# Two decode layers on one core: w1 streamed in each layer, one pool, and a whole group's K kept across the layers

## The chip, the cores and the metric

The kernel runs on one core of a Trainium2 chip. The metric is the device time of one execution in microseconds; the number shown for a kernel is the median of several executions. All sizes are float32. Where the text says MiB it means 2^20 bytes; GB/s are 10^9 bytes per second.

## The reference

Two layers, each an attention block over a cache and a gated feed-forward block, for four rows of one token each:

```python
def _A_ref(x, k_cache, v_cache, wq, wo):          # B=4, D=512, 32 query heads, 8 groups, 4096 positions, 128 wide
    q = (x @ wq).reshape(B, Sq, Hq, Dh).transpose(0, 2, 1, 3)
    k = jnp.repeat(k_cache, rep, axis=1)
    v = jnp.repeat(v_cache, rep, axis=1)
    p = _softmax(jnp.einsum("bhqd,bhkd->bhqk", q, k) * (Dh ** -0.5), axis=-1)
    o = jnp.einsum("bhqk,bhkd->bhqd", p, v)
    return o.transpose(0, 2, 1, 3).reshape(B, Sq, Hq * Dh) @ wo

def _B_ref(x, w1, w3, w2):                         # F = 1792
    return (_silu(x @ w1) * (x @ w3)) @ w2

x = A_x
x = x + _A_ref(_layernorm(x), k_cache, v_cache, wq, wo)
x = x + _B_ref(_layernorm(x), w1, w3, w2)
x = x + _A_ref(_layernorm(x), k_cache, v_cache, wq, wo)
x = x + _B_ref(_layernorm(x), w1, w3, w2)
```

Both layers read the same caches and the same weights. Each cache is 64 MiB, wq and wo are 8 MiB each, w1, w3 and w2 are 3.5 MiB each.

## The kernel before, in words

**Steps.** A layer goes through the 8 groups; each group has 4 steps of 1024 positions. A step needs 2 MiB of K and 2 MiB of V (all four rows of the batch). The first layer takes the groups 0 to 7, the second 7 to 0, so group 7 (`TURN`) is the last of the first layer and the first of the second. In a step TensorE computes the scores (L320), VectorE takes the maximum (L323), ScalarE the exponent (L340), TensorE turns the result (L346) and multiplies it with V (L370). The scores of the next step stand ahead of the rest of the step before it.

**The tail of a layer.** Behind the last V come the output projection (L397), a layernorm (L252 to L277) and the feed-forward block: w3's first 256 of 448 columns (L413), w1 (L420), w3's other 192 columns (L413), the gate (L423, L425, L428), five transposes (L432 to L434), and w2 in five pieces of 4, 4, 4, 1 and 1 rows (L446). `busy(n)` puts n transposes of a constant on TensorE whose result nobody reads (L246); they stand in the tail between the real operations.

**What is loaded, and in which order.** `plan` is a list of all loads, in the order of need. `pump()` walks it: a load of a weight that has its own home is issued at once; any other takes a place in `free` (first fit) and, when no place is large enough, the walk stops there until `done()` or `vacate()` gives a place back. So the order of the loads never changes, and a late release holds up every load behind it. All loads stand on SyncE's queue (SPq in the profile). Each load also takes one of eight completion semaphores in turn (DMAHW0 to DMAHW7 in the rows of order below), so SyncE issues a load only once the eighth before it has landed.

**Where it lands.** `pages` has 17 places of 512 KiB. wq and wo (but for group 0's share) have homes of their own; in the second layer the parts that are no longer needed are added to `free`. w1 has a home (3.5 MiB), is loaded once in two halves in the first layer (beside groups 2 and 4) and read by both layers. w3 and w2 are streamed through `free` in both layers.

**What is kept for the second layer.** Of group 7's 16 pages of K nine stay in `pages` (`KEPT`: steps 2 and 3 and one page of step 1), and one (`STORED`) is copied to PSUM by ScalarE (L317) and copied back in the second layer (L176). The other six are loaded again. The second layer takes group 7's steps in the order 2, 3, 0, 1.

Of the kernel before, what the change touches and what calls it, by code (L numbers as in the profile page):

```python
# [8 lines left out]
F32 = mybir.dt.float32  # L9
# [14 lines left out]
FJ = F // 4  # L24
FW = (256, FJ - 256)
EPS = 1e-5
SCALE = DH ** -0.5
RT = 4 * U
# [16 lines left out]
def tile_decode_layers(ctx: ExitStack, tc: tile.TileContext, x, kt, v, wq, wo, w1, w3, w2, out):  # L45
# [18 lines left out]


    homes = {"pages": pages, "wq": wq_sb.rearrange("p g k n -> p (g k n)"),
             "wo": wo_sb.rearrange("p g h e -> p (g h e)")}
    free = [("pages", 0, PAGES)]

# [19 lines left out]

    def stream(keys, src, n=None):  # L90
        plan.append((keys, src, len(keys) if n is None else n))

    def keep(dst, src):
        plan.append((None, src, dst))

    def cache(which, layer, g, c, parts=(4,)):
        src = (kt if which == "k" else v)[g, c]
        r = 0
        for n in parts:
            keys = [(which, layer, g, c, r + i) for i in range(n)]  # L100
            if which == "k" and g == TURN and layer and (c, r) in KEPT:
                pass
            elif layer and keys[0] == ("k", layer, TURN, *STORED):
                stream(keys, None)
            else:
                stream(keys, src[:, r * U:(r + n) * U])
            r += n

    def parts_of(which, layer, i, g, c):
        if which == "k" and g == TURN and c == 1:  # L110
            return (2, 1, 1)
        if i == len(orders[layer]) - 1:
            return (2, 1, 1)
        if layer == 0 and i == len(orders[layer]) - 2 and which == "v":
            return (2, 2)
        if layer == 0 and i == 0:
            return (1, 1, 2)
        if layer and i < 4:
            return (2, 2) if (c, 0) not in KEPT or which == "v" else (4,)
        return (4,)  # L120

    def wq_load(a, b):
        keep(wq_sb[:, a:b].rearrange("p g k n -> p (g k n)"), wq[:, a * RT // 2:b * RT // 2])

    def wo_load(a, b):
        keep(wo_sb[:, a - 1:b - 1].rearrange("p g h e -> p (g h e)"), wo[:, a * RT // 2:b * RT // 2])

    for layer in range(LAYERS):
        steps = orders[layer]
        if layer == 0:  # L130
            wq_load(0, 1)
        for i, (g, c) in enumerate(steps):
            if which_parts := parts_of("k", layer, i, g, c):
                cache("k", layer, g, c, which_parts)
            if layer == 0 and c == 1:
                if g in (0, 1, 3, 5):
                    wq_load(*{0: (1, 2), 1: (2, 4), 3: (4, 6), 5: (6, 8)}[g])
                elif g in (2, 4):
                    k = g - 2
                    keep(w1_sb[:, k:k + 2].rearrange("p k f -> p (k f)"), w1[:, k * F:(k + 2) * F])  # L140
            if i:
                cache("v", layer, *steps[i - 1], parts_of("v", layer, i - 1, *steps[i - 1]))
            if layer == 0 and c == 2:
                if g == 0:
                    stream([("wo", 0)], wo[:, 0:RT // 2], 2)
                elif g in (1, 3, 5):
                    wo_load(g, g + 2)
        cache("v", layer, *steps[-1], parts_of("v", layer, len(steps) - 1, *steps[-1]))
        if layer == 0:
            wo_load(TURN, HKV)  # L150
        else:
            stream([("wo", 1)], wo[:, 0:RT // 2], 2)
        for u in range(2):
            for k in (0, 2):
                a = 4 * KC * FW[0] * u + 4 * FW[u] * k
                stream([("w3", layer, u, k), ("w3", layer, u, k + 1)], w3[:, a:a + 8 * FW[u]])
        for i, (a, b) in enumerate(W2_PARTS):
            stream([("w2", layer, i)], w2[:, a * D:b * D], (b - a + 1) // 2)

# [3 lines left out]
    def pump():  # L163
        while state["next"] < len(plan):
            keys, src, n = plan[state["next"]]
            if keys is None:
                nc.sync.dma_start(n, src)
            else:
                got = take(n)
                if got is None:  # L170
                    return
                home, at, _ = got
                dst = homes[home][:, at * U:(at + n) * U]
                if src is None:
                    for i in range(2):
                        nc.scalar.activation(dst[:, i * U // 2:(i + 1) * U // 2], stored[i], AF.Copy)  # L176
                else:
                    width = src.shape[-1]
                    nc.sync.dma_start(dst[:, :width], src)
                    assert width % len(keys) == 0  # L180
                    n = width // len(keys)
                left[state["next"]] = len(keys)
                room[state["next"]] = got
                for i, key in enumerate(keys):
                    where[key] = (dst[:, i * n:(i + 1) * n] if src is not None else dst, state["next"])
# [95 lines left out]
    def project_q(layer, g, xT, rq):  # L281
        pq = misc()

        def product(k):
            for h in range(REP):
                nc.tensor.matmul(pq[32 * h:32 * h + 32, 0, :], xT[:, 32 * k:32 * k + 32],  # L286
                                 wq_sb[:, g, k, h * DH:(h + 1) * DH], start=(k == 0), stop=(k == KC - 1))

        def turn_q():
            pt = misc()  # L290
            nc.tensor.transpose(pt[:, 0, :], q, ident)
            nc.vector.tensor_copy(qT[:, :, 0:REP],
                                  pt[:, 0, :].rearrange("p (h b) -> p b h", h=REP)[:, 0:B, :])

        product(0)
        yield
        product(1)
        yield
        product(2)
        product(3)  # L300
        if layer:
            vacate("wq", 2 * g, 2)
# [90 lines left out]
    def project_o(layer, g, rowsum):  # L393
# [7 lines left out]
        elif layer:  # L401
            vacate("wo", 2 * g - 2, 2)
        nc.vector.scalar_tensor_tensor(x_sb, x_ps, 1.0, x_sb, op0=ALU.mult, op1=ALU.add,
                                       accum_out=rowsum)

    def feed_forward(layer, xT, rstd, rowsum):
        pg, pu = scores(0), scores(1)

        def up(u):
            for k in range(KC):  # L410
                w = loaded("w3", layer, u, k)
                for j in range(4):
                    nc.tensor.matmul(pu[32 * j:32 * j + 32, FW[0] * u:FW[0] * u + FW[u]], xT[:, 32 * k:32 * k + 32],  # L413
                                     w[:, j * FW[u]:(j + 1) * FW[u]], start=(k == 0), stop=(k == KC - 1))
                done("w3", layer, u, k)
# [135 lines left out]
```

## Time and profile before

| what | us |
|---|---|
| median of 3 runs | 724.01 (723.31 to 724.14) |
| the profiled execution, its own time | 723.5 |
| its span, first to last instruction | 721.6 |
| TensorE busy | 472.6 (65%) |
| VectorE busy | 194.8 (27%) |
| ScalarE busy | 120.1 (17%) |
| moved by DMA | 300.67 MB, mean 417 GB/s |

The profiled execution is 0.5 us faster than the median; between its span and its time lie 1.9 us. Busy times overlap, so no engine's sum is the time.

### The profile page before, as it was taken

To read this page: it belongs to the slowest core of one execution; us is meant where nothing else is said; L and a number is where in the kernel's file an instruction comes from. 1 tells how busy PE (TensorE), PEld (TensorE's weight loads), DVE (VectorE), ACT (ScalarE), POOL (GpSimd) and SP (SyncE) were. 2 spreads that over 40 slices of the span, in tenths; PEclk is the share of its full clock that TensorE was granted. 3 is DMA by queue.
4 is the path that set the end of the run, shared out by engine and by line. 5 is a ranking of instruction groups with operands and counts; after the bars stand their busy time and mean duration, and the time that the engine had idled before them with its cause. 6 is when DMAs were issued, how large, how long until landed. Compare 5 with 4: busy or idle time off the path is not lost.

```text
span 721.6 us, 18367 instructions
## 1 busy us (share of the span) xinstructions
PE 472.6 (65%) x8310; PEld 300.5 (42%) x8310; DVE 194.8 (27%) x694; ACT 120.1 (17%) x323; POOL 2.9 (0%) x10
## 2 busy tenths in 40 slices
PE   5664665745566755566678766766667667566778
PEld 3342443423334533334455544444444444344455
DVE  2222122231122312323222432222332232322221
ACT  1111111111011101112121311111111111111121
POOL 0000000000000000000000000000000000000000
PEclk9887688998678968989999999899998988998799
DMA  9999999999999999999999999999999999999995
GB/s 363 427 430 422 430 424 428 425 426 427 428 422 429 426 429 425 428 423 423 412 371 402 424 426 425 428 425 428 423 430 424 427 427 424 427 426 425 423 416 221
DMA packets 25853, 300.67 MB, mean 417 GB/s; under 512 B 2864, under 2 KB 3120, under 8 KB 5936
## 3 DMA queue, kind: packets, MB, share of 16 engines
q1 hardware_dynamic: 25632, 299.45, 98.5%
q8 instruction: 65, 1.06, 0.6%
q14 instruction: 12, 0.10, 0.0%
q10 hardware_dynamic: 144, 0.07, 0.0%
HBM read 299.43 MB, written 0.07 MB: 415 GB/s over the span
## 4 chain that ended last, share of the span: by engine, by line
DMA 81%; PE 16%; DVE 1%; issue 1%; SPq 0%; ACT 0%; DVEq 0%; ACTq 0%
DMA pages<-in_v 44%; DMA pages<-in_kt 28%; PE sums_ps L370 6%; DMA pages<-in_w 5%; PE scores L320 5%; DMA wq_sb<-in_v 4%; PE turned L346 2%; PE misc L286 1%; DVE pT L348 1%; PE sums_ps L446 0%; PE scores L420 0%; DVE stat L323 0%; PE scores L246 0%; PE scores L413 0%; PE sums_ps L397 0%
## 5 line engine op out<-in xcount | busy, mean ns | idle before, releaser
L370 PE MATMUL sums_ps<-pages,pT 128*4 128x128 f32 x3152 | 128.5, 306 | 127.0 <-DMA pages<-in_v 101.1
L320 PE MATMUL scores<-pages,qT 128*32 128x256 f32 x1736 | 125.0, 436 | 56.5 <-DMA pages<-in_kt 49.9
L370 PEld LDWEIGHTS sums_ps<-pages,pT 128*4 128x4 f32 x3152 | 82.0, 94 | 162.5 <-issue 99.4
L340 ACT ACTIVATE p<-scores,stat 128x512 f32<-128x512 f32 x128 | 87.0, 680 | 282.1 <-PE turned L346 220.4
L323 DVE TENSOR_REDUCE stat<-scores 128x1 f32<-128x512 f32 x128 | 88.5, 691 | 139.4 <-PE scores L320 139.3
L320 PEld LDWEIGHTS scores<-pages,qT 128*32 128x32 f32 x1736 | 63.9, 123 | 99.8 <-issue 74.2
L346 PE MATMUL turned<-ident,p 128*128 128x128 f32 x512 | 95.3, 315 | 0.0
L348 DVE COPY pT<-turned 128x64 f32<-128x64 f32 x128 | 28.1, 219 | 245.7 <-PE turned L346 245.5
L346 PEld LDWEIGHTS turned<-ident,p 128*128 128x128 f32 x512 | 61.1, 156 | 47.7 <-issue 44.9
L335 ACT ACTIVATE stat<-stat 128x1 f32<-128x1 f32 x48 | 14.1, 295 | 269.2 <-DVE stat L333 269.2
L370 PE MATMUL sums_ps<-wq_sb,pT 128*4 128x128 f32 x672 | 25.2, 294 | 24.1 <-DMA wq_sb<-in_v 20.0
L370 PEld LDWEIGHTS sums_ps<-wq_sb,pT 128*4 128x4 f32 x672 | 17.1, 91 | 30.6 <-issue 20.3
L286 PE MATMUL misc<-wq_sb,xT 128*32 128x128 f32 x512 | 24.7, 297 | 0.7 <-DVE ve L275 0.4
L340 ACT ACTIVATION_READ_ACCUMULATOR p<-scores,stat 128x1 f32 x128 | 24.5, 192 | 0.0
L397 PE MATMUL sums_ps<-wo_sb,oT 128*4 128x128 f32 x448 | 15.6, 283 | 6.1 <-DVE o L379 5.4
L246 PE MATMUL scores<-ident 128*128 128x128 f32 x104 | 18.1, 300 | 1.9 <-POOL ident masks.py:199 1.4
L286 PEld LDWEIGHTS misc<-wq_sb,xT 128*32 128x32 f32 x512 | 16.6, 120 | 1.2 <-ACT xT L268 0.4
L370 PE MATMUL sums_ps<-wo_sb,pT 128*4 128x128 f32 x272 | 10.8, 284 | 9.5 <-DMA wo_sb<-in_v 8.0
L397 PEld LDWEIGHTS sums_ps<-wo_sb,oT 128*4 128x4 f32 x448 | 10.8, 88 | 11.3 <-DVE o L379 9.9
L381 DVE SCALAR_TENSOR_TENSOR o<-o,stat,sums_ps 128x128 f32<-128x128 f32 x32 | 11.0, 343 | 13.9 <-PE sums_ps L370 13.9
L246 PEld LDWEIGHTS scores<-ident 128*128 128x128 f32 x104 | 11.8, 148 | 5.6 <-issue 2.4
L320 PE MATMUL scores<-wq_sb,qT 128*32 128x256 f32 x192 | 11.5, 380 | 2.3 <-DMA wq_sb<-in_kt 2.3
(81 smaller groups left out, 187.5 us busy)
## 6 DMA issues: line engine op xcount, KB each, us to landing
pages<-in_kt SPq DMA_DIRECT2D x47, 2048.0 KB, 18.9
pages<-in_v SPq DMA_DIRECT2D x43, 2048.0 KB, 19.5
wq_sb<-in_v SPq DMA_DIRECT2D x9, 2048.0 KB, 32.9
wq_sb<-in_kt SPq DMA_DIRECT2D x6, 2048.0 KB, 32.8
pages<-in_v SPq DMA_DIRECT2D x10, 1024.0 KB, 10.2
wo_sb<-in_v SPq DMA_DIRECT2D x4, 2048.0 KB, 34.1
pages<-in_w SPq DMA_DIRECT2D x7, 1024.0 KB, 11.1
pages<-in_kt SPq DMA_DIRECT2D x6, 1024.0 KB, 9.8
```

Of the source, the lines that this page charges most:

```text
L246: nc.tensor.transpose(pt[:, 0:P], ident, ident)
L286: nc.tensor.matmul(pq[32 * h:32 * h + 32, 0, :], xT[:, 32 * k:32 * k + 32], wq_sb[:, g, k, h * DH:(h + 1) * DH], start=(k == 0), stop=(k = ...
L320: nc.tensor.matmul(ps[32 * b:32 * b + 32, r * QC:(r + 1) * QC], qT[:, b, :], t[:, b, :], start=True, stop=True)
L323: nc.vector.tensor_reduce(st["stat"][:, h:h + 1], ps, axis=AX.X, op=ALU.max, negate=True)
L335: nc.scalar.activation(stat[:, 6:7], stat[:, 2:3], AF.Exp, bias=stat[:, 3:4], scale=-1.0)
L340: nc.scalar.activation(st["p"].rearrange("p n s -> p (n s)"), st["ps"][h], AF.Exp, bias=stat[:, 3:4], accum_out=stat[:, 4 + h:5 + h])
L346: nc.tensor.transpose(pt[:, n, :], st["p"][:, n, :], ident)
L348: nc.vector.tensor_copy(pT, pt.rearrange("p n (b h) -> p n b h", b=B)[:, :, :, 0:REP])
L370: nc.tensor.matmul(o_ps[32 * b:32 * b + REP, :], st["pT"][h][:, NT * (r % 2) + n, b, :], t[:, b, n, :], start=(r == 0 and n == 0), stop=(r ...
L381: nc.vector.scalar_tensor_tensor(acc["o"], acc["o"], st["stat"][:, 6:7], o_ps, op0=ALU.mult, op1=ALU.add)
L397: nc.tensor.matmul(x_ps[32 * k:32 * k + B, :], oT[:, h, :], w[:, h, k * P:(k + 1) * P], start=(h == 0), stop=(h == REP - 1))
```

## The change

Five things change together. w1 loses its home and is streamed in both layers behind the last V, in four pieces of 896 KiB (one for each quarter of the 512 inputs), ahead of w3, which now comes in four such pieces too. `pages` (17 places of 512 KiB) becomes `pool` (96 places of 128 KiB, 24 of the old ones), so pieces take what they need in steps of 128 KiB. All of group 7's K but the `STORED` page (now the last of step 3) stays in the pool for the second layer: 15 pages and the one in PSUM, so none is loaded again, and the second layer takes the steps in their plain order. TensorE computes w1's product first, then w3's whole product. And which loads are cut into smaller pieces changes a little: V of the last three steps of the first layer and of the first two of the second.

```diff
-PAGES = 17
+KB = 256
+POOL = 96
 TURN = HKV - 1
-KEPT = {(2, 0): 4, (3, 0): 4, (1, 3): 1}
-STORED = (1, 2)
+STORED = (STEPS - 1, 3)
...
-    pages = const.tile([P, PAGES * U], F32, name="pages")
+    pool = const.tile([P, POOL * KB], F32, name="pool")
...
-    w1_sb = const.tile([P, KC, F], F32, name="w1_sb")
...
-        orders.append([(g, c) for i, g in enumerate(groups)
-                       for c in ((2, 3, 0, 1) if layer and i == 0 else range(STEPS))])
+        orders.append([(g, c) for g in groups for c in range(STEPS)])
...
-    free = [("pages", 0, PAGES)]
+    free = [("pool", 0, POOL)]
...
-                elif g in (2, 4):
-                    k = g - 2
-                    keep(w1_sb[:, k:k + 2].rearrange("p k f -> p (k f)"), w1[:, k * F:(k + 2) * F])
...
-        for u in range(2):
-            for k in (0, 2):
-                a = 4 * KC * FW[0] * u + 4 * FW[u] * k
-                stream([("w3", layer, u, k), ("w3", layer, u, k + 1)], w3[:, a:a + 8 * FW[u]])
+        for name, w in (("w1", w1), ("w3", w3)):
+            for k in range(KC):
+                stream([(name, layer, k)], w[:, k * F:(k + 1) * F])
...
-                    if key[0] == "k" and key[2] == TURN and key[1] == 0:
-                        for (c, r), m in KEPT.items():
-                            if key[3] == c and r <= key[4] < r + m:
-                                where[("k", 1, *key[2:])] = where[key]
-                                kept.add(key)
+                    if key[:3] == ("k", 0, TURN) and key[3:] != STORED:
+                        where["k", 1, *key[2:]] = where[key]
+                        kept.add(key)
...
-        up(0)
-        for k in range(KC):
-            for j in range(4):
-                nc.tensor.matmul(pg[32 * j:32 * j + 32, 0:FJ], xT[:, 32 * k:32 * k + 32],
-                                 w1_sb[:, k, j * FJ:(j + 1) * FJ], start=(k == 0), stop=(k == KC - 1))
+                    nc.tensor.matmul(ps[32 * j:32 * j + 32, 0:FJ], xT[:, 32 * k:32 * k + 32],
+                                     w[:, j * FJ:(j + 1) * FJ], start=(k == 0), stop=(k == KC - 1))
+                done(name, layer, k)
+
+        product("w1", pg)
         gate = work.tile([P, FJ], F32, name="gate", tag="p", bufs=1)
...
-        up(1)
+        product("w3", pu)
```

On SyncE's queue at the turn from the first layer to the second, before (behind wo's last piece; widths are in floats of each of 128 partitions, so 2048 is 1 MiB; `in_w3` is w3 in device memory):

```order
L167 DMA wo_sb_70<-in_wo 128x2048
L179 DMA pages_68<-in_w3 128x2048 x2
L179 DMA pages_68<-in_w3 128x1536 x2
L179 DMA pages_68<-in_w2 128x2048 x3
L179 DMA pages_68<-in_w2 128x512 x2
L179 DMA pages_68<-in_v 128x2048 x2
L179 DMA pages_68<-in_kt 128x2048 x2
L179 DMA wq_sb_69<-in_v 128x2048
L179 DMA pages_68<-in_v 128x2048
L179 DMA pages_68<-in_kt 128x2048
```

The same place after the change:

```order
L154 DMA wo_sb_70<-in_wo 128x2048
L165 DMA pool_68<-in_w1 128x1792 x4
L165 DMA pool_68<-in_w3 128x1792 x4
L165 DMA pool_68<-in_w2 128x2048 x3
L165 DMA pool_68<-in_w2 128x512 x2
L165 DMA pool_68<-in_v 128x2048 x4
L165 DMA pool_68<-in_v 128x4096
L165 DMA pool_68<-in_kt 128x4096
```

Four pieces of w1 stand ahead of w3, the three K pieces of group 7 are gone, and behind w2 come four halves of V and then V of the third step in one piece of 2 MiB. By the pool's bookkeeping the four w3 pieces each take the place of the w1 piece of the same number, the first two of w2 wait for w3's second piece, the last three of w2 and the first V half for w3's fourth, the other V halves for w2's first three pieces, and the 2 MiB V piece for the scores of the second layer's first step.

On TensorE in the feed-forward block of the first layer, before (`scores1` collects w3's product, `scores0` w1's):

```order
L413 MATMUL scores1_3099<-pages_68,xT_3083 32x256 x16
L420 MATMUL scores0_3098<-w1_sb_71,xT_3083 32x448 x16
L413 MATMUL scores1_3099<-pages_68,xT_3083 32x192 x16
L246 MATMUL scores0_3158<-ident_84 128x128 x7
L432 MATMUL turned_3166<-ident_84,gate_3134 128x128 x3
```

The same place after it:

```order
L396 MATMUL scores0_3094<-pool_68,xT_3079 32x448 x16
L396 MATMUL scores1_3095<-pool_68,xT_3079 32x448 x16
L229 MATMUL scores0_3143<-ident_85 128x128 x7
L411 MATMUL turned_3151<-ident_85,gate_3116 128x128 x3
L412 MATMUL turned_3151<-ident_85,gate_3116 128x128
```

w3's product is no longer parted around w1's, and nothing on TensorE stands between the pieces of either weight.

## Rows read from the trace of the kernel before

**Rows 1.** The page: GB/s in 40 slices of the span, and the chain that ended last.
```profile
GB/s 363 427 430 422 430 424 428 425 426 427 428 422 429 426 429 425 428 423 423 412 371 402 424 426 425 428 425 428 423 430 424 427 427 424 427 426 425 423 416 221
DMA 81%; PE 16%; DVE 1%; issue 1%; SPq 0%; ACT 0%; DVEq 0%; ACTq 0%
```

**Rows 2.** Timeline of SyncE's queue near the end: start us, us, what was issued.
```profile
642.20 0.33 SPq L179 DMA_DIRECT2D wq_sb<-in_v  x1
...
656.84 0.33 SPq L179 DMA_DIRECT2D wo_sb<-in_kt  x1
662.53 5.22 SPq L179 DMA_DIRECT2D wq_sb<-in_v  x2
...
682.12 0.33 SPq L179 DMA_DIRECT2D pages<-in_wo  x1
684.61 0.33 SPq L179 DMA_DIRECT2D wq_sb<-in_w  x1
```

**Rows 3.** Timeline of TensorE at the end: start us, us, instructions, [idle before <-what ended it].
```profile
692.11 1.83 PE L370 MATMUL sums_ps<-wq_sb,pT 128*4 128x128 f32 x32 [3.29 <-DMA wq_sb<-in_v]
...
704.68 1.07 PE L413 MATMUL scores<-wq_sb,xT 128*32 128x256 f32 x16
...
706.43 3.19 PE L420 MATMUL scores<-w_sb,xT 128*32 128x448 f32 x32
709.44 1.48 PE L413 MATMUL scores<-wo_sb,xT 128*32 128x192 f32 x32
...
713.04 1.06 PE L446 MATMUL sums_ps<-wo_sb,hT 128*4 128x128 f32 x32
...
716.44 1.06 PE L446 MATMUL sums_ps<-pages,hT 128*4 128x128 f32 x32 [0.18 <-DMA pages<-in_w]
```

**Rows 4.** Windows at the turn and behind it: us, busy by engine, PEclk, DMA share, GB/s.
```profile
374.00:388.00 14.00, 12.87 (x204) 7.85 (x204) 2.56 (x9) 2.40 (x4) 0.55 (x1) 1.00 0.89 344
400.00:420.00 20.00, 16.88 (x361) 11.49 (x354) 8.34 (x29) 5.96 (x17) 0.00 (x0) 1.00 1.01 422
```

**Rows 5.** Timeline at the turn: TensorE's waits for weights, ScalarE, and the second layer's first scores.
```profile
376.62 1.07 PE L413 MATMUL scores<-pages,xT 128*32 128x256 f32 x16 [0.18 <-DMA pages<-in_w]
...
388.35 1.06 PE L446 MATMUL sums_ps<-pages,hT 128*4 128x128 f32 x32 [1.02 <-DMA pages<-in_w]
...
389.92 0.62 PE L446 MATMUL sums_ps<-pages,hT 128*4 128x128 f32 x16
...
392.25 0.28 ACT L268 ACTIVATE xT<-turned 128x128 f32<-128x128 f32 x1 [9.26 <-PE turned L265]
...
395.18 1.94 PE L320 MATMUL scores<-pages,qT 128*32 128x256 f32 x32 [0.27 <-DVE qT L292]
...
399.65 0.60 ACT L176 ACTIVATE pages<-stored 128x512 f32<-128x512 f32 x1 [0.72 <-PE scores L320]
```

**Rows 6.** A load at the turn on SyncE's queue, and half-microsecond windows behind it.
```profile
376.49 0.33 SPq L179 DMA_DIRECT2D pages<-in_w  x1
...
377.00:377.50 0.50, 0.50 (x16) 0.26 (x8) 0.00 (x0) 0.00 (x0) 0.00 (x0) 1.00 0.96 274
...
379.00:379.50 0.50, 0.50 (x12) 0.24 (x8) 0.00 (x0) 0.00 (x0) 0.00 (x0) 1.00 1.05 438
```

**Rows 7.** Windows and TensorE's timeline around two stretches in which it waited.
```profile
22.60:26.60 4.00, 1.77 (x42) 1.22 (x36) 0.58 (x3) 0.78 (x2) 0.00 (x0) 1.00 1.03 438
26.70:30.00 3.30, 0.42 (x5) 0.25 (x9) 0.00 (x0) 0.00 (x0) 0.00 (x0) 0.50 1.00 427
504.50:507.80 3.30, 1.52 (x35) 0.89 (x33) 1.60 (x7) 0.78 (x2) 0.00 (x0) 1.00 0.97 412
508.00:511.00 3.00, 3.00 (x32) 1.52 (x31) 0.69 (x1) 0.00 (x0) 0.00 (x0) 0.50 1.00 423
...
507.88 3.61 PE L320 MATMUL scores<-pages,qT 128*32 128x256 f32 x32 [1.07 <-DMA pages<-in_kt]
```

**Rows 8.** Timeline of TensorE: the first instruction after a long wait.
```profile
662.60 1.89 PE L370 MATMUL sums_ps<-pages,pT 128*4 128x128 f32 x32 [3.12 <-DMA pages<-in_v]
```

More of the change, by code (lines that the diff above doesn't have):

```diff
@@ L88, in tile_decode_layers, with stream, cache @@
     plan = []
-    def stream(keys, src, n=None):
-        plan.append((keys, src, len(keys) if n is None else n))
+    def stream(keys, src):
+        plan.append((keys, src, None))
     def keep(dst, src):
         plan.append((None, src, dst))
-    def cache(which, layer, g, c, parts=(4,)):
+    def cache(which, layer, i, g, c):
         src = (kt if which == "k" else v)[g, c]
+        last = i == len(orders[layer]) - 1
+        if which == "k" and (g, c) == (TURN, STORED[0]):
+            parts = (2, 1, 1)
+        elif last:
+            parts = (2, 1, 1)
+        elif layer == 0 and i == 0:
+            parts = (1, 1, 2)
+        elif which == "v" and ((layer == 0 and i >= len(orders[0]) - 3) or (layer and i < 2)):
+            parts = (2, 2)
+        else:
+            parts = (4,)
         r = 0
         for n in parts:
[L100 to L104, printed above, removed]
+            keys = [(which, layer, g, c, r + j) for j in range(n)]
+            if which == "k" and g == TURN and layer:
+                if (c, r) == STORED:
+                    stream(keys, None)
             else:
@@ L107, in cache @@
             r += n
[L109 to L120, printed above, removed]
     def wq_load(a, b):
-        keep(wq_sb[:, a:b].rearrange("p g k n -> p (g k n)"), wq[:, a * RT // 2:b * RT // 2])
+        keep(wq_sb[:, a:b].rearrange("p g k n -> p (g k n)"), wq[:, a * 2 * U:b * 2 * U])
     def wo_load(a, b):
-        keep(wo_sb[:, a - 1:b - 1].rearrange("p g h e -> p (g h e)"), wo[:, a * RT // 2:b * RT // 2])
+        keep(wo_sb[:, a - 1:b - 1].rearrange("p g h e -> p (g h e)"), wo[:, a * 2 * U:b * 2 * U])
     for layer in range(LAYERS):
@@ L132, in tile_decode_layers @@
         for i, (g, c) in enumerate(steps):
[L133 to L137, printed above, removed]
-                elif g in (2, 4):
-                    k = g - 2
-                    keep(w1_sb[:, k:k + 2].rearrange("p k f -> p (k f)"), w1[:, k * F:(k + 2) * F])
+            cache("k", layer, i, g, c)
+            if layer == 0 and c == 1 and g in (0, 1, 3, 5):
+                wq_load(*{0: (1, 2), 1: (2, 4), 3: (4, 6), 5: (6, 8)}[g])
             if i:
-                cache("v", layer, *steps[i - 1], parts_of("v", layer, i - 1, *steps[i - 1]))
+                cache("v", layer, i - 1, *steps[i - 1])
             if layer == 0 and c == 2:
                 if g == 0:
-                    stream([("wo", 0)], wo[:, 0:RT // 2], 2)
+                    stream([("wo", 0)], wo[:, 0:2 * U])
                 elif g in (1, 3, 5):
                     wo_load(g, g + 2)
-        cache("v", layer, *steps[-1], parts_of("v", layer, len(steps) - 1, *steps[-1]))
+        cache("v", layer, len(steps) - 1, *steps[-1])
         if layer == 0:
@@ L151, in tile_decode_layers @@
         else:
[L152 to L156 removed]
+            stream([("wo", 1)], wo[:, 0:2 * U])
+        for name, w in (("w1", w1), ("w3", w3)):
+            for k in range(KC):
+                stream([(name, layer, k)], w[:, k * F:(k + 1) * F])
         for i, (a, b) in enumerate(W2_PARTS):
[L158 removed]
+            stream([("w2", layer, i)], w2[:, a * D:b * D])
     state = {"next": 0}
@@ L164, in pump @@
         while state["next"] < len(plan):
-            keys, src, n = plan[state["next"]]
+            keys, src, dst = plan[state["next"]]
             if keys is None:
-                nc.sync.dma_start(n, src)
+                nc.sync.dma_start(dst, src)
             else:
-                got = take(n)
+                width = U if src is None else src.shape[-1]
+                got = take(width // KB)
                 if got is None:
                     return
-                home, at, _ = got
-                dst = homes[home][:, at * U:(at + n) * U]
+                dst = homes[got[0]][:, got[1] * KB:got[1] * KB + width]
                 if src is None:
@@ L184, in pump @@
                 for i, key in enumerate(keys):
-                    where[key] = (dst[:, i * n:(i + 1) * n] if src is not None else dst, state["next"])
-                    if key[0] == "k" and key[2] == TURN and key[1] == 0:
-                        for (c, r), m in KEPT.items():
-                            if key[3] == c and r <= key[4] < r + m:
-                                where[("k", 1, *key[2:])] = where[key]
-                                kept.add(key)
+                    where[key] = dst[:, i * n:(i + 1) * n], state["next"]
+                    if key[:3] == ("k", 0, TURN) and key[3:] != STORED:
+                        where["k", 1, *key[2:]] = where[key]
+                        kept.add(key)
             state["next"] += 1
@@ L407, in feed_forward, with product @@
         pg, pu = scores(0), scores(1)
[L409 removed]
+        def product(name, ps):
             for k in range(KC):
[L411 removed]
+                w = loaded(name, layer, k)
                 for j in range(4):
[L413 to L421 removed]
+                    nc.tensor.matmul(ps[32 * j:32 * j + 32, 0:FJ], xT[:, 32 * k:32 * k + 32],
+                                     w[:, j * FJ:(j + 1) * FJ], start=(k == 0), stop=(k == KC - 1))
+                done(name, layer, k)
+        product("w1", pg)
         gate = work.tile([P, FJ], F32, name="gate", tag="p", bufs=1)
```

19 lines of the change are left out of this document (6 added, 13 removed).

## The prediction

> **What bounds the kernel now.** I read the page first. The chain that ended last is 81% DMA, and 34 of 40 slices move 420 GB/s or more; the exceptions are the start, the turn between the layers and the end [rows 1]. So the load stream is the bound, and a change is worth what it adds to or takes from that stream, plus what it does at the three places where the stream is not full. Next I read SyncE's queue, because with eight semaphores in turn the spacing of its issues is the spacing of landings. From 642.20 to 656.84 lie three pieces of 2 MiB, 4.88 us each; behind a piece of 1 MiB the spacing is 2.49 [rows 2]. So a piece costs 2.44 to 2.49 us per MiB and the small one pays almost nothing extra. Now and then a spacing is longer: 5.69 at 662.53 [rows 2].
>
> At the end the reader should see two chains that meet. TensorE waits for V until 692.11, then works its way through the tail, 12.6 us to the feed-forward block at 704.68, and waits once more, 0.18 us, for w2's third piece at 716.44 [rows 3]. The stream is the later one, but only just: the end stands on that landing, and TensorE has no slack to lose.
>
> **The bytes.** Removed: three K pieces of 1 MiB, 3 x 2.49 = 7.5 us. Added: w1 a second time, four pieces of 0.875 MiB. No row shows that size; it lies between 2.14 us by the rate of the 2 MiB pieces and 2.18 by that of the 1 MiB pieces [rows 2]. I take 2.17, as it is nearer to 1 MiB: 8.7 us. Cutting the first w1 load and leaving some K and V pieces whole moves 0.1 us each way. Sum **+1.2 us** (1.0 to 1.4). Nothing hides it, since the stream is full; that it moves from the first layer to behind the last V only brings every V of the layers forward by the same 8.7 us.
>
> **The turn before.** Between 374 and 388 the stream moves 344 GB/s, against 422 later [rows 4]: 14 x (1 - 344/422) = 2.6 us on the mean of the sixteen engines. But a load has landed only when its slowest engine is done. From w3's second piece (376.62) to w2's third (388.35) TensorE's waits mark two landings [rows 5]; 4.5 MiB at 2.49 are 11.2 us, and it took 11.7. So the landings lose **0.5 us**, and the rest of the dip is faster engines that wait. The bounds are 0 (one long spacing as at 662.53 would explain it alone) and 2.6. If the changed turn had no gap it would win that much.
>
> **The turn after.** The pool has 24 places of 512 KiB, 15 of them kept, so 9 are left, against 8 before. w1 fills 7 and leaves 2 in scraps, which no w3 piece fits. So w3 waits for w1's products, w2 for w3's. These releases come early enough: TensorE reads w1's first piece as soon as xT is there, while three w1 pieces still have to land. The tight one is the V of the second layer's third step. It needs a 2 MiB stretch, and gets it when the first step's scores are done. Before, that was 395.18 + 1.94 = 397.1, which is 8.8 us after w2's third piece landed at 388.3 [rows 5]. After the change the stream has 0.5 MiB of w2 and four 1 MiB pieces of V behind that landing: 4.5 x 2.49 = 11.2 us. If TensorE is no later than before, the issue leads the stream's end by 11.2 - 8.8 - 0.1 = 2.3 us.
>
> How much lead a load needs shows at 376.49, where one was issued into a queue that had begun to drain: the engines are at work from 377.0 (0.5 us later), the bytes are back at full rate in the window from 379.0 (2.5 us later) [rows 6]. Bounds 0.5 and 2.5; I take 2.5, since bytes are what the stream is made of. So this place costs 0.2 us if TensorE is as fast as before, and for each microsecond that it is later, one more.
> The Trainium skill (DMA: Bandwidth & Descriptors, Anatomy of one DMA) gives a fixed cost of about 2.0 us per DMA; as an estimate by that figure the place would cost 0.5 us less than by mine, and the sum below would be 726.2.
>
> **TensorE's clock in the tail.** w1's product takes 3.19 us for its four quarters [rows 3], 0.80 each. A quarter now lands every 2.17 us. By the spacing of the landings, w1's third piece already comes after TensorE has caught up: in the last layer w1 is whole 17.4 us before the stream's end, w3 8.7 us, and TensorE reaches the block 34.3 - 12.6 = 21.7 us before the end. So for about 10 us TensorE works 0.80 of every 2.17 us, in gaps of 1.4 us, with no `busy` in them.
> What such a stretch does to the clock: before 26.6 TensorE was busy 1.77 of 4.0 us, and from 26.7 the granted clock is 0.50, which is 1.2 of 2.4 GHz; before 507.8 it was busy 1.52 of 3.3, with no gap over 1.07 us ahead of the instruction at 507.88, and again 0.50 follows [rows 7]. The new stretch is emptier than both. So I expect the lower level when w3's last quarter lands. At that level a group of 32 takes 1.89 us [rows 8] and 1.06 at the higher [rows 3]: a factor of 1.78.
> The Trainium skill (TensorE: Matmul & The Clock Gate, HAM oscillation) has as its rule that long idle gaps of TensorE are what to avoid; gaps of 1.4 us would be harmless by it, which is the first rival below. The rows at 507 don't agree with that reading, since the clock fell there behind gaps no longer than that.
>
> **The end after.** From w3's last landing, 8.7 us before the stream's end, TensorE has a quarter (0.80), then 2.1 us up to w2 (709.44 + 1.48 to 713.04), then two parts of w2 at 1.6 us each to the third (713.04 to 716.44 less the wait) [rows 3]. At the higher clock it begins that third part 8.7 - 0.8 - 2.1 - 3.2 = 2.6 us before the stream's end, ahead of its landing 1.24 us before it (0.5 MiB follow), and the end stands where it did. At the lower clock the quarter and the 2.1 us take 1.78 times as long, 5.2 us: w2 begins 3.5 us before the stream's end, its third part 0.3 us before it. That is **0.9 us** late, if w2 itself runs at the higher clock again, as such groups do in steady work [rows 3]; TensorE has no gap in those 5.2 us. Bounds: 0.2, if the clock comes back halfway, and 5 if all of w2 stays at the lower level. The same 0.9 us come at the turn, where they take the lead from 2.3 to 1.4 us: **1.1 us** lost (0 to 1.1 by the bounds of the lead).
>
> **At no cost.** ScalarE's copies of the stored page now stand ahead of the second layer's xT: 2 x 0.60 us between w2's end (390.5) and xT (392.25) [rows 5], 0.5 us to spare. Without that cover they'd delay the first scores, and so the tight V. In the last tail places are plenty, and the loads are held by the eight semaphores alone.
>
> **Sum.** 723.5 + 1.2 - 0.5 + 1.1 + 0.9 = 726.2 on the profiled execution. That one lies 0.5 under the median, so **726.7**. Below 0.2% (1.4 us) a measurement can hardly tell a change of this kernel from none.
>
> **The rivals.** (1) The clock stays up, since the matmuls of the new stretch are long ones of 448 columns and no row has just such a stretch. Then 723.5 + 1.2 - 0.5 + 0.2 + 0.5 = 724.9: no change to be measured. For it: the clock was 1.00 all through the old block [rows 4]; against it: rows 7. (2) Faster: the dip at the turn counts with its mean and closes. 723.5 + 1.2 - 2.6 + 0.5 = 722.6. It needs the clock up, the V lead enough, and landings that follow the mean of the engines; the 11.7 us speak against it. It decides from the point at which the turn gives back more than the 1.2 us of bytes. (3) w2 stays at the lower clock in both layers: 5 us at the end and 3 or more at the turn, where no lead is left: 732. For it: after 692.11 a whole group still ran at 1.83 [rows 3]; against it: steady work lies ahead of w2.
>
> **How the numbers follow.** My forecast has 0.64, with 725.0 to 729.2 as its own range (the end at 0.2 to 3, the turn before at 0 to 1.2). Rival 1 has 0.22, rival 2 0.06, rival 3 0.08. The range 724.2 to 729.2 leaves out rivals 2 and 3 and little else. Faster 0.06; slower 0.66, the forecast's upper part and rival 3; same 0.28, rival 1 and the forecast's low end.
>
> **What would show it.** Right: a granted clock of 0.5 in both feed-forward blocks while w1 and w3 land; TensorE waiting for pool pieces between quarters; w2's third part that no longer waits at the end; a wait for V in the second layer's third step and a dip of GB/s some 20 us behind the turn; feed-forward blocks some 21 us ahead of the stream's end. Wrong: a clock of 1.00 there, w2's third part still waiting for its load, or a stream whose spacing for 0.875 MiB is not 2.17.

## The result and the profile after

The changed kernel takes **727.35 us** (median of 5 runs, 726.86 to 727.76) against 724.07 (723.31 to 724.59) in the same session: a ratio of 1.0045, 95% interval [1.003, 1.006]. It is slower by 3.3 us; the prediction had 726.7. The profiled execution took 727.45, its span is 725.7 us, 4.1 more than before.

The page of the changed kernel, the same two lines as [rows 1]:

```profile
GB/s 364 429 426 425 426 427 426 425 427 427 427 424 426 430 425 426 425 426 419 416 356 391 378 429 424 428 427 425 425 426 427 425 427 426 426 426 424 417 418 228
DMA 86%; PE 12%; DVE 1%; issue 1%; SPq 0%; ACT 0%; ACTq 0%; DVEq 0%
```

The stream is still the bound. What differs is the turn: three slices (356, 391, 378) where before had two (371, 402). TensorE at the turn, answering to [rows 5]:

```profile
362.77 1.06 PE L380 MATMUL sums_ps<-wo_sb,oT 128*4 128x128 f32 x32 [0.65 <-DMA wo_sb<-in_wo]
...
371.35 0.96 PE L396 MATMUL scores<-pool,xT 128*32 128x448 f32 x8 [1.20 <-DMA pool<-in_w]
373.55 0.96 PE L396 MATMUL scores<-pool,xT 128*32 128x448 f32 x8 [1.24 <-DMA pool<-in_w]
375.72 1.72 PE L396 MATMUL scores<-pool,xT 128*32 128x448 f32 x8 [1.22 <-DMA pool<-in_w]
377.91 1.72 PE L396 MATMUL scores<-pool,xT 128*32 128x448 f32 x8 [0.47 <-DMA pool<-in_w]
380.05 1.72 PE L396 MATMUL scores<-pool,xT 128*32 128x448 f32 x8 [0.42 <-DMA pool<-in_w]
...
385.72 1.06 PE L425 MATMUL sums_ps<-pool,hT 128*4 128x128 f32 x32 [0.21 <-DMA pool<-in_w]
...
388.93 1.06 PE L425 MATMUL sums_ps<-pool,hT 128*4 128x128 f32 x32 [1.56 <-DMA pool<-in_w]
...
396.11 1.93 PE L303 MATMUL scores<-pool,qT 128*32 128x256 f32 x32 [0.27 <-DVE qT L275]
...
438.32 1.06 PE L353 MATMUL sums_ps<-pool,pT 128*4 128x128 f32 x32 [2.09 <-DMA pool<-in_v]
```

Each row that ends a wait for DMA marks a landing, so they are the clock of the stream. The quarters of w1 and w3 land 2.14 to 2.20 us apart, as the 2.17 of the prediction. Then it goes wrong: from w3's last quarter (380.05) to w2's second piece (385.72) lie 2 MiB and 5.67 us; the third piece, 1 MiB, takes another 3.21 (388.93). At 2.49 per MiB these would be 4.98 and 2.49.

Windows of the changed kernel at the turn (columns as [rows 4]):

```profile
364.00:368.00 4.00, 3.65 (x44) 1.94 (x42) 0.95 (x6) 0.28 (x1) 0.55 (x1) 1.00 0.72 299
368.00:372.00 4.00, 1.75 (x20) 0.31 (x16) 0.00 (x0) 0.00 (x0) 0.00 (x0) 1.00 0.94 359
372.00:376.00 4.00, 1.54 (x16) 0.36 (x16) 0.69 (x1) 2.12 (x3) 0.00 (x0) 0.95 1.02 425
376.00:380.00 4.00, 3.16 (x16) 0.20 (x8) 0.00 (x0) 0.00 (x0) 0.00 (x0) 0.50 0.91 343
...
384.00:388.00 4.00, 3.15 (x72) 2.21 (x64) 0.05 (x1) 0.00 (x0) 0.00 (x0) 1.00 0.94 316
...
396.00:400.00 4.00, 2.02 (x36) 1.02 (x40) 1.59 (x4) 0.78 (x2) 0.00 (x0) 1.00 1.01 350
...
408.00:412.00 4.00, 3.08 (x76) 2.30 (x78) 1.46 (x7) 1.74 (x5) 0.00 (x0) 1.00 0.92 303
```

There are five dips where before had one long one. The first (299, then 359) costs the landings nothing: the quarters that land at 371.35, 373.55 and 375.72 keep their spacing. The later ones do cost, though the fourth (350, at 396 to 400) not the load whose late issue stands in it, as the account below shows. And the granted clock has fallen to 0.50 in the fourth window.

SyncE's issues at the later dips, and the second and third scores of the second layer on TensorE:

```profile
377.45 0.33 SPq L165 DMA_DIRECT2D pool<-in_w  x1
...
381.79 0.33 SPq L165 DMA_DIRECT2D pool<-in_w  x1
...
398.10 0.33 SPq L165 DMA_DIRECT2D pool<-in_v  x1
401.91 0.33 SPq L165 DMA_DIRECT2D pool<-in_kt  x1
407.85 0.33 SPq L165 DMA_DIRECT2D pool<-in_v  x1
...
399.91 1.93 PE L303 MATMUL scores<-pool,qT 128*32 128x256 f32 x32 [1.87 <-ACT p L323]
405.88 1.91 PE L303 MATMUL scores<-pool,qT 128*32 128x256 f32 x32
```

Each stands at the end of a TensorE row: 375.72 + 1.72 = 377.44 is the end of w3's second quarter at the lower clock, and w2's first piece is issued then; 380.05 + 1.72 = 381.77 is the same for w3's fourth quarter and w2's third piece; 396.11 + 1.93 = 398.04 for the second layer's first scores and the V of the third step. The K and the V behind it follow the ends of the next two scores (401.84 and 407.79). Loads wait for places, and places for TensorE.

The clock, in windows around both feed-forward blocks, answering to [rows 7]:

```profile
375.70:382.40 6.70, 5.79 (x27) 1.30 (x28) 0.53 (x1) 0.00 (x0) 0.00 (x0) 0.50 0.96 375
382.50:390.00 7.50, 5.72 (x118) 4.33 (x117) 0.49 (x4) 0.00 (x0) 0.00 (x0) 1.00 0.97 360
...
710.20:716.90 6.70, 6.07 (x29) 3.07 (x30) 0.68 (x1) 0.00 (x0) 0.00 (x0) 0.50 0.84 347
717.00:722.50 5.50, 5.50 (x128) 3.96 (x126) 0.44 (x3) 0.00 (x0) 0.00 (x0) 1.00 0.27 107
```

Both blocks have the stretch at 0.50, the level of 1.2 GHz, and both are back at 2.4 for w2. TensorE at the end, answering to [rows 3]:

```profile
687.93 1.89 PE L353 MATMUL sums_ps<-pool,pT 128*4 128x128 f32 x32 [4.01 <-DMA pool<-in_v]
...
701.33 3.47 PE L396 MATMUL scores<-wq_sb,xT 128*32 128x448 f32 x32
...
710.40 1.72 PE L396 MATMUL scores<-wq_sb,xT 128*32 128x448 f32 x8 [1.23 <-DMA wq_sb<-in_w]
712.55 1.72 PE L396 MATMUL scores<-wo_sb,xT 128*32 128x448 f32 x8 [0.43 <-DMA wo_sb<-in_w]
...
717.33 1.06 PE L425 MATMUL sums_ps<-wo_sb,hT 128*4 128x128 f32 x32
...
720.47 1.06 PE L425 MATMUL sums_ps<-wo_sb,hT 128*4 128x128 f32 x32
```

w2's third piece (720.47) no longer waits for its load: TensorE has become the later of the two chains.

### The profile page after: what moved, and what is told of

It reads as the page before. It is cut to its first block, busy times and chain, and to the rows that moved or that the text cites. A ratio compares the mean times of both kernels' runs of the same rounds, so it can differ in the third digit from the quotient of the medians.

```text
span 725.7 us, 18239 instructions
## 1 busy us (share of the span) xinstructions
PE 474.8 (65%) x8246; PEld 298.8 (41%) x8246; DVE 195.1 (27%) x694; ACT 120.2 (17%) x323; POOL 2.9 (0%) x10
## 3 DMA queue, kind: packets, MB, share of 16 engines
q8 instruction: 65, 1.06, 0.6%
## 4 chain that ended last, share of the span: by engine, by line
DMA 86%; PE 12%; DVE 1%; issue 1%; SPq 0%; ACT 0%; ACTq 0%; DVEq 0%
DMA pool<-in_v 45%; DMA pool<-in_kt 21%; DMA wo_sb<-in_v 6%; DMA wq_sb<-in_v 5%; PE sums_ps L353 4%; DMA pool<-in_w 4%; PE scores L303 3%; DMA pool<-in_wo 2%; DMA wo_sb<-in_w 2%; PE turned L329 1%; PE scores L229 1%; PE scores L396 1%; PE sums_ps L425 1%; DVE stat L306 0%; PE misc L269 0%
## 5 line engine op out<-in xcount | busy, mean ns | idle before, releaser
L353 PE MATMUL sums_ps<-pool,pT 128*4 128x128 f32 x3552 | 143.1, 303 | 132.2 <-DMA pool<-in_v 107.6
L353 PEld LDWEIGHTS sums_ps<-pool,pT 128*4 128x4 f32 x3552 | 91.5, 93 | 171.2 <-issue 101.2
L303 PE MATMUL scores<-pool,qT 128*32 128x256 f32 x1760 | 118.3, 413 | 58.2 <-DMA pool<-in_kt 52.7
L303 PEld LDWEIGHTS scores<-pool,qT 128*32 128x32 f32 x1760 | 62.2, 117 | 97.1 <-issue 68.5
L353 PE MATMUL sums_ps<-wq_sb,pT 128*4 128x128 f32 x320 | 11.9, 288 | 9.3 <-DMA wq_sb<-in_v 7.7
L303 PE MATMUL scores<-wq_sb,qT 128*32 128x256 f32 x176 | 14.0, 466 | 3.5 <-DMA wq_sb<-in_kt 3.5
L396 PE MATMUL scores<-pool,xT 128*32 128x448 f32 x64 | 9.8, 700 | 5.6 <-DMA pool<-in_w 5.6
## 6 DMA issues: line engine op xcount, KB each, us to landing
pool<-in_kt SPq DMA_DIRECT2D x49, 2048.0 KB, 29.5
```

Of the source, the lines that this page charges most:

```text
L303: nc.tensor.matmul(ps[32 * b:32 * b + 32, r * QC:(r + 1) * QC], qT[:, b, :], t[:, b, :], start=True, stop=True)
L353: nc.tensor.matmul(o_ps[32 * b:32 * b + REP, :], st["pT"][h][:, NT * (r % 2) + n, b, :], t[:, b, n, :], start=(r == 0 and n == 0), stop=(r ...
L396: nc.tensor.matmul(ps[32 * j:32 * j + 32, 0:FJ], xT[:, 32 * k:32 * k + 32], w[:, j * FJ:(j + 1) * FJ], start=(k == 0), stop=(k == KC - 1))
```

## The account of the stretch behind the turn

One yardstick serves for all kernels. It runs from the landing of wo's last piece to a landing some 55 us or more later at which TensorE again waits. The MiB in between come from the order of the loads, and the yardstick is the time above 2.46 us per MiB, a rate between the 2.44 of the large pieces and the 2.49 of 1 MiB [rows 2]. In the kernel before, these two rows of TensorE:

```profile
371.79 1.06 PE L397 MATMUL sums_ps<-wo_sb,oT 128*4 128x128 f32 x32 [0.65 <-DMA wo_sb<-in_wo]
...
428.06 1.93 PE L320 MATMUL scores<-pages,qT 128*32 128x256 f32 x32 [2.63 <-DMA pages<-in_kt]
```

They enclose 22 MiB and 56.27 us: 2.1 above 54.1. In the changed kernel, 362.77 to 438.32 enclose 28.5 MiB (7 of w1 and w3, 3.5 of w2, 4 of V in halves, seven pieces of 2) and 75.55 us: 5.4 above 70.1. **The turn got 3.3 us worse.** The table has the same number for the kernels below. It is read in the profiled execution, whose own time stands beside the median, as the two can differ.

| kernel | working places of 512 KiB | from, to | MiB | us | above 2.46 per MiB | profiled execution | median |
|---|---|---|---|---|---|---|---|
| before | 8 | 371.79, 428.06 | 22 | 56.27 | 2.1 | 723.5 | 724.07 |
| after | 9 | 362.77, 438.32 | 28.5 | 75.55 | 5.4 | 727.45 | 727.35 |
| busy_first | 9 | 363.03, 436.83 | 28.5 | 73.80 | 3.7 | 726.25 | 726.59 |
| v_halves | 9 | 363.06, 441.02 | 30.5 | 77.96 | 2.9 | 725.99 | 725.69 |
| best | 9 | 363.43, 441.31 | 30.5 | 77.88 | 2.8 | 725.59 | 725.14 |
| fine_best | 9 | 363.45, 440.68 | 30.5 | 77.23 | 2.2 | 726.27 | 725.01 |
| keep12 | 12 | 362.63, 428.43 | 26 | 65.80 | 1.8 | 727.03 | 727.31 |
| before_room | 12 | 371.72, 432.81 | 24 | 61.09 | 2.1 | 729.17 | 729.11 |
| best16 | 8 | 362.98, 438.98 | 28 | 76.00 | 7.1 | 727.54 | 724.91 |
| fine17 | 7 | 363.29, 446.14 | 29.5 | 82.85 | 10.3 | 730.43 | 729.66 |

Which loads of the changed kernel were late can be read without TensorE. Each load makes sixteen increments on its semaphore in the trace, and the sixteenth is its landing. Three loads behind w2 (the V of the third step, the K behind it, the V of the fourth step; what was issued, how often, KB, us from issue to landing):

```profile
pool<-in_v SPq DMA_DIRECT2D x1, 2048.0 KB, 7.7
pool<-in_kt SPq DMA_DIRECT2D x1, 2048.0 KB, 10.2
pool<-in_v SPq DMA_DIRECT2D x1, 2048.0 KB, 10.8
```

Issued at 398.10, 401.91 and 407.85, they land at 405.85, 412.08 and 418.62 by the increments, and the load ahead of them at 400.92. So the V of the third step took 4.92 us for its 2 MiB, as such a piece does in steady work, and lost nothing. The K behind it took 6.24 and the next V 6.54, together 3.0 us too long. The first, third and fourth pieces of w2 lose 0.7, 0.7 and 0.9 in the same way, and all other loads up to 438.32 next to nothing.

Part of this is there whatever the kernel. Far from any turn, too, some spacings are longer: in the changed kernel TensorE's waits for V and K end at 646.89, 652.34 and 658.34, so 5.45 and 6.00 for 2 MiB in place of 4.89, 1.7 us in all. By the increments such losses recur in every trace, in keep12 most plainly: its landings at 126.45, 216.06, 310.72, 397.71, 473.80, 553.77 and 638.34 come 1.5 to 1.6 us late each. The one at 397.71 is all that its stretch loses, and one of 1.4 most of what the stretch of fine_best loses. The changed kernel has none between 325 and 488 but for its turn. So, as an estimate, about 1.6 of its 5.4 is one of these and some 3.8 is its own. What makes these losses is open. The 65 instruction packets of a run (16 KB and about 1 us each, one in some 11 us) use the same DMA engines and could be behind them, but most are followed by no late landing, and no run varies them.

## The experiments

**Clock in the first block (busy_first) and in the last (busy_last).** Idle transposes between the quarters, in one layer each:

```
                 done(name, layer, k)
+                if layer == 0 and (name, k) not in (("w1", 0), ("w3", KC - 1)):
+                    pt = turned()
+                    for _ in range(6):
+                        nc.tensor.transpose(pt[:, 0, :], ident, ident)
```

(`layer == 1` in the second.) Expected:

> The changed kernel with six idle transposes behind each quarter of w1 and w3 but the first and the last, in the first layer alone. Theory (the lower clock of TensorE delays the releases at the turn): granted clock 1.00 in the first feed-forward block, w2's first and third piece issued some 0.8 us earlier, 1.0 to 1.4 us of the turn's loss gone, so 726.0 to 726.4 us against 727.4 of the changed kernel. Rival (the turn loses because nine places are too few, whatever TensorE's clock): 727.4, within 0.4.

> The same transposes in the second layer alone. Theory (the end is 0.5 us late because of the clock): w2's third part waits for its load again, 0.5 us less, 726.9 us. Rival (the end stands on the load stream alone): 727.4 and the same distance from the last landing to the end.

Measured: busy_first 726.59 (726.25 to 727.28), ratio to before 1.0035 [1.0023, 1.0047]; busy_last 726.87 (725.89 to 727.77), 1.0036 [1.0023, 1.0049]. TensorE in busy_first, with the same three landings as above:

```profile
380.31 0.96 PE L396 MATMUL scores<-pool,xT 128*32 128x448 f32 x8 [0.39 <-DMA pool<-in_w]
...
385.27 1.06 PE L429 MATMUL sums_ps<-pool,hT 128*4 128x128 f32 x32 [0.46 <-DMA pool<-in_w]
387.97 1.06 PE L429 MATMUL sums_ps<-pool,hT 128*4 128x128 f32 x32 [1.06 <-DMA pool<-in_w]
...
436.83 1.06 PE L353 MATMUL sums_ps<-pool,pT 128*4 128x128 f32 x32 [0.75 <-DMA pool<-in_v]
```

Its window and SyncE's issue of w2's first piece:

```profile
375.70:382.40 6.70, 5.62 (x46) 2.79 (x47) 0.69 (x1) 0.00 (x0) 0.00 (x0) 1.00 1.02 414
```
```profile
376.94 0.33 SPq L165 DMA_DIRECT2D pool<-in_w  x1
```

At the full clock w2's first piece is issued 3.4 us ahead of the landing before it (380.31), where it was 2.6 (377.45 to 380.05). The 2 MiB up to 385.27 take 4.96, nothing lost, and the third 2.70. So by the yardstick the clock costs 1.7 us at the turn, 1.2 of them on w2's first three pieces, and it does so by the places that TensorE gives back late. By the medians it is 0.8, with ranges that overlap. From 387.97 on, the loss of 3.3 us (18.5 MiB in 48.86) stays: that is not the clock's.

In busy_last the end answers:

```profile
711.99 0.96 PE L396 MATMUL scores<-wo_sb,xT 128*32 128x448 f32 x8 [0.42 <-DMA wo_sb<-in_w]
714.82 1.06 PE L429 MATMUL sums_ps<-wo_sb,hT 128*4 128x128 f32 x32
...
719.38 1.06 PE L429 MATMUL sums_ps<-wo_sb,hT 128*4 128x128 f32 x32 [0.83 <-DMA wo_sb<-in_w]
```

w2's third piece waits again, 7.39 us behind w3's last landing. In the changed kernel that landing would be at 712.55 + 7.39 = 719.94 (719.90 by the increments), and TensorE came at 720.47: 0.5 us late. The medians differ by 0.5 as well, but their ranges overlap, so this rests on the rows.

**V in halves for two more steps (v_halves).**

```
-        elif which == "v" and (... or (layer and i < 2)):
+        elif which == "v" and (... or (layer and i < 4)):
```

> The changed kernel with V of the second layer's third and fourth step in halves of 1 MiB, which go into the 1 MiB places that come free earlier. Theory (at the turn a V piece waits for a whole 2 MiB place, the tight place of the prediction): 1.1 us less by the prediction's figure, up to 3 us if all loss between 396 and 416 us of the trace is that wait, so 724.5 to 726.3. Rival (the loss there is not the place but other traffic or the earlier weights): 727.4, within 0.4.

Measured: 725.69 (724.54 to 727.21, 12 runs), 1.0022 [1.0013, 1.0032]: 1.7 us faster than the changed kernel. TensorE:

```profile
388.87 1.06 PE L425 MATMUL sums_ps<-pool,hT 128*4 128x128 f32 x32 [1.01 <-DMA pool<-in_w]
...
441.02 1.34 PE L303 MATMUL scores<-pool,qT 128*32 128x256 f32 x20 [1.07 <-DMA pool<-in_kt]
```

Behind w2's third piece 20.5 MiB take 52.15, 1.7 above the yardstick, where the changed kernel loses 3.9 (18.5 MiB from 388.93 to 438.32, 49.39 us). A V in halves doesn't need a stretch of 2 MiB, and its halves are issued from 395.18, not 398.10. Which loads it was the increments show: the K and the V of the fourth step, 3.0 us late in the changed kernel, are 0.0 late here, while w2's third and fourth pieces still lose 1.0 and 1.1.

**Room and bytes (keep12, before_room, bytes15).** keep12 keeps three pages fewer, so that 1.5 MiB are read again and 12 places work:

```
+                elif c == STORED[0]:
+                    stream(keys, src[:, r * U:(r + n) * U])
...
-                    if key[:3] == ("k", 0, TURN) and key[3:] != STORED:
+                    if key[:3] == ("k", 0, TURN) and key[3] != STORED[0]:
```

before_room does the like to the kernel before (`KEPT = {(3, 0): 4, (1, 3): 1}`), and bytes15 loads 1.5 MiB in the middle of the second layer of the changed kernel, which nothing reads:

```
+            if layer and i == 14:
+                stream([("extra", 0)], kt[0, 0][:, 0:3 * U])
```

> The changed kernel with 12 instead of 15 pages of group 7 kept in the pool, so three K pages (1.5 MiB) are loaded again and 12 places are left at the turn instead of 9. Bytes alone: 1.5 x 2.49 = 3.7 us more, 731.1. Theory (room at the turn is worth some 2 to 3 us): 728.0 to 729.2, with no dip of GB/s behind the turn.

> The kernel before with one fewer group of pages kept (4 pages, 2 MiB, read again; 12 working places in place of 8). The bytes cost 2 MiB x 2.49 us = 5.0 us. If the turn of before loses little for want of places, as the prediction had it (0.5 us), 724.07 + 5.0 - 0.5 = 728.6. If it loses some 2 us, 727.0.

> The changed kernel with three more 512 KiB pages loaded in the middle of the second layer, which nothing reads. If loads are the bound there and every byte is on the path, 1.5 MiB x 2.49 us = 3.7 us more: 731.1. If there is slack in the stream there, less: 727.4 to 729. It prices the 1.5 MiB that the kernel with three fewer kept pages read again without being slower.

Measured: keep12 727.31 (727.02 to 727.85), 1.0043 [1.0032, 1.0055]; before_room 729.11 (727.94 to 729.33), 1.0069 [1.0057, 1.0082]; bytes15 731.02 (730.55 to 732.42), 1.0098 [1.0082, 1.0113].

bytes15 is 3.7 us above the changed kernel, 2.45 per MiB: in mid layer every byte is on the path. keep12 carries the same 3.7 and is level with the changed kernel, so three places more gave 3.7 us back. For w2's pieces room is the only difference; the pages read again stand ahead of the V of the third step (landings at 402.50 and 403.77), so the loads behind them gain lead by these bytes too, and what room alone gave them isn't separated. TensorE in keep12:

```profile
379.93 1.72 PE L398 MATMUL scores<-pool,xT 128*32 128x448 f32 x8 [0.44 <-DMA pool<-in_w]
387.40 1.06 PE L427 MATMUL sums_ps<-pool,hT 128*4 128x128 f32 x32 [0.21 <-DMA pool<-in_w]
428.43 1.06 PE L355 MATMUL sums_ps<-pool,pT 128*4 128x128 f32 x32 [1.44 <-DMA pool<-in_v]
```

Its clock is the lower one too (1.72), and still the three pieces of w2 take 7.47, nothing lost: with room, the clock is harmless at the turn. before_room is the counterpart: four places more gave the kernel before nothing that can be measured (5.0 us of bytes; 5.1 us slower, 4.1 to 5.9 by the interval). Its dip of 344 GB/s [rows 4] was never worth 2.6 us, nor the 2 that the other reading allowed.

**Repairs together (best, fine_best).** best has both edits of idle transposes and the halves of V. fine_best adds pages half as long (`KB = 128`, `POOL = 192`) and w1 and w3 in eighths of 448 KiB.

> The changed kernel with idle transposes behind the pieces of w1 and w3 in both layers and with V of the second layer's third and fourth step in halves. If the three gains are separate (first layer's clock 0.8, last layer's clock 0.5, places of V 1.7), 727.35 - 3.0 = 724.4, which is level with before (724.1). Rival: the first layer's clock and the halves mend the same loss at the turn, and only the larger counts: 727.35 - 1.7 - 0.5 = 725.2.

> As the kernel with halves of V and idle transposes in both layers, with the pool cut into pages half as long and w1 and w3 moved in eighths of 448 KiB in place of quarters: places come free after half as much work, so that w3's and w2's loads are issued earlier. If what is still lost at the turn (the first and third pieces of w2, about 1 to 2 us on landings) is lead, 723.0 to 724.0; if twice the number of smaller transfers costs more than the lead gives, 725 or more.

Measured: best 725.14 (724.45 to 726.89, 11 runs), 1.0019 [1.001, 1.0028]; fine_best 725.01 (724.67 to 726.49, 9 runs), 1.002 [1.0011, 1.003]. So best meets its rival: the first layer's clock and the halves mend the same loss. Their yardsticks are 2.8 and 2.2, and the 1.0 to 1.1 us that are left to the kernel before are about the price of the bytes.

**One page kept more (fine16, fine17, fine16z, best16).** Quarters of a V of the last group stay for the second layer, in fine_best or in best:

```
+AGAIN = (0, 3)
...
+            elif which == "v" and g == TURN and layer and c == AGAIN[0] and r >= AGAIN[1]:
+                pass
...
+                            or key[:4] == ("v", 0, TURN, AGAIN[0]) and key[4] >= AGAIN[1]):
```

> The kernel with pages half as long, w1 and w3 in eighths, halves of V and idle transposes, with one more page kept: the last quarter of V of the last group's first step is not read again. That takes 0.5 MiB off the stream, 1.25 us. If the turn still has places enough with 8 in place of 9: 725.0 - 1.25 = 723.8, level with before (724.1). If the ninth place was worth more than its bytes: 725 or above.

> As the one before, with two more pages of that V kept, 7 working places: 725.0 - 2.5 = 722.5 if places are still enough, which would be faster than before. If the turn loses 1 us or more for each place, as the changed kernel does, 725 or above.

> One more page kept, 8 working places, but of V of the last group's last step, which is the last load of the first layer's attention and is freed later in the second layer. Same bytes: 723.8 if only bytes count; above the kernel that keeps V of the first step if it matters when a place comes free behind the turn.

> Whole pages and quarters of w1 and w3, with halves of V and idle transposes, and the last quarter of V of the first step kept: 725.1 - 1.25 = 723.9 if 8 places are enough. With w1 in quarters of 1.75 pages 8 places leave a scrap of one page: if scraps matter, above the same kernel with eighths by more than 0.5 us.

Measured: fine16 726.86 (725.64 to 728.17), 1.0045 [1.0032, 1.0058]; fine17 729.66 (726.42 to 730.74), 1.0073 [1.0054, 1.0092]; fine16z 726.47 (725.29 to 728.96), 1.004 [1.0027, 1.0052]; best16 724.91 (723.77 to 728.33, 11 runs), 1.0022 [1.0008, 1.0036]. None beats the kernel before. TensorE in fine17:

```profile
388.09 1.06 PE L439 MATMUL sums_ps<-pool,hT 128*4 128x128 f32 x32 [0.86 <-DMA pool<-in_w]
393.60 1.89 PE L439 MATMUL sums_ps<-pool,hT 128*4 128x128 f32 x32 [3.87 <-DMA pool<-in_w]
```

Two landings of 1 MiB lie 5.5 us apart, 3.0 of them lost for want of a place. From 9 to 8 to 7 places the medians of the fine kernel (fine_best, fine16, fine17) go 725.0, 726.9, 729.7, while each step takes 1.25 us of bytes away: a place is worth 3 to 4 us there, more than twice its bytes. fine16z is no worse than fine16, so when the page comes free in the second layer doesn't decide it; and quarters are no worse than eighths, since best16 is the lowest of the four. The coarse kernel (best) pays less for the place: best and best16 are each 1.1 us slower than the kernel before in their own session, so that the ninth place was worth about the page's 1.25. But its times spread over 4.6 us, and the profiled one (727.54), whose yardstick reads 7.1, is among the longer.

## Why the prediction was right, and where its sum was wrong

**The bytes** (+1.2): right. The quarters land 2.17 us apart, and bytes15 has the price of a MiB at 2.45.

**The clock**: right in place and level. It fell in both blocks behind gaps of 1.20 to 1.24 us and came back for w2; the old block had no such stretch, and in busy_first six idle transposes behind each quarter but the first and the last kept it at 1.00. Rival 3 needed w2 at the lower clock, and its groups take 1.06. By the rule of the Trainium skill (TensorE: Matmul & The Clock Gate, HAM oscillation) it is long idle gaps that have to be avoided, and by that these would have done no harm; the rows at 375.72 and 710.40 don't agree. Another section of that page of the Trainium skill (TensorE: Matmul & The Clock Gate, A second HAM failure mode) tells of a kernel in which brief idling between groups of matmuls was enough, and with that they do agree.

**The end** (+0.9): right in mechanism, 0.5 in size. From w3's last quarter to w2 TensorE takes 4.78 (712.55 to 717.33) against 2.83 in busy_last, 1.95 more where the prediction had 2.3.

**The turn before** (-0.5): nothing speaks against it. before_room rules out the 2.6, but can't tell 0.5 from 0.

**The turn after** (+1.1): this term failed, in size and in place. With the gain of 0.5 the prediction had the turn 0.6 worse; it was 3.3. Two of its steps are wrong. "These releases come early enough", said of w1's and w3's places, fell: w2's first and third pieces were late, each issued at the end of a product at the lower clock, for 1.4 us up to 388.93. And "The tight one is the V of the second layer's third step" put the loss on one load. In the changed kernel that V was issued 2.8 us ahead of the landing before it and lost nothing. Nor did TensorE wait for it, which was one of the signs named: between 396.11 and 438.32 no row of TensorE waits for a load. The K and the V behind it lost 3.0 us. In busy_first, by the increments, it is the V that loses 1.1 and the K nothing, so which load pays differs from kernel to kernel; halving the V of two steps gave 2.2 us back by the yardstick. The prediction looked at each load's lead by itself. The runs show one shortage, of places, which passes from load to load: keep12 shows its size (3.7 us, with the reservation made there), busy_first and v_halves mend parts of it that overlap.

As to the lead that a load needs, the prediction took 2.5 us as if one number did. From issue to the landing of the piece ahead, 2.6 (377.45 to 380.05) lost 0.7 and 3.4 in busy_first lost nothing; but 3.9 (381.79 to 385.72) lost 0.7 again. The Trainium skill (DMA: Bandwidth & Descriptors, Anatomy of one DMA) has a fixed cost of about 2.0 us per DMA. It gives that for DMAs that GpSimd issues, and these are SyncE's; taken as their lead, as the prediction's estimate took it, it would have had both late loads in time, and they were not.

**The sum.** 1.2 for bytes, 3.3 at the turn and 0.5 at the end are 5.0, and the spans differ by 4.1. Most of the remainder is in the last layer: from V's landing to w2's third piece before, 692.11 to 716.44 [rows 3], 9.5 MiB took 24.33, 1.0 above the yardstick; after, from 687.93 to w3's last quarter at 712.55, 10 MiB took 24.62, nothing above it. By the increments 0.6 of that 1.0 is one landing before, w2's first piece at 711.46, which came 3.11 us behind the one ahead. Losses of that kind recur in all the kernels, so I count it as chance where they fall, which is argued and not shown. So the forecast had the bytes, the clock and the end right by their mechanisms, and the turn's direction. That the sum came so close is partly luck: what it missed at the turn (2.7) was made up for in part by 0.4 too much at the end, by this 1.0, and by 0.6 that it added from the profiled execution to the median (0.5, where the changed kernel's profiled execution lies 0.1 above its median).

**The rivals.** Rival 1 (the clock stays up, 724.9) was wrong twice: the clock fell, and where idle transposes held it up in the first block the time was still 726.59. Rival 2 (the dip closes) fell: the dip grew.

## What to carry to other kernels

When weights are moved from a home of their own into a pool, count the places that the pool has left at the moment when a stage consumes slowly, not only the bytes: here 1.2 us were bytes, and three more places gave back 3.7. Follow every load behind the turn to the instruction that frees its place, with that instruction's clock, and add their lateness up; one tight load is seldom alone. And test places and bytes apart: a load that nothing reads prices the bytes, fewer kept pages price the room.

## What was not expected of the hardware

A dip of the mean rate and a late landing are two things. In the changed kernel 364 to 372 lost 1.8 us on the mean (299 and 359 against 424 GB/s) and landings none; of the later dips all but the one at 396 to 400 came with late landings. From the first of a load's sixteen increments to the last one sees how far the fastest engine is ahead of the slowest. For the load ahead of the one issued at 367.43 that is 5.6 us; for the one ahead of the issue at 377.45 it is 1.8. The dip at 396 to 400 takes it from 2.1 to 1.0 us and costs no landing; the next one does. In keep12 it stays between 4.1 and 6.7 us over the whole stretch. So I read it that a dip first uses up the head start of the faster engines, and the next ones fall on the slowest. The kernel before had one deep dip, the changed one five. This was argued from the traces and not tested by itself.

With few places the time also scatters: best16 ran from 723.77 to 728.33 on the chip on which the kernel before ran from 722.83 to 725.55.
